# Splitting the last 512 bytes off four large loads of a decode kernel

## The chip, the cores and the metric

The kernel runs on one core of a Trainium2 chip. The core has a matrix engine (PE, with its weight loads shown as PEld), a vector engine (DVE), a scalar engine (ACT), a general engine (POOL) and a sequencer that only issues and waits (SP). Sixteen DMA engines move data between the chip's memory (HBM) and the core's on-chip memory of 128 partitions. A transfer is issued by an instruction on one of the queues and is done when every DMA engine that carries a part of it is done. The metric is the device time of one execution in microseconds; a smaller number is better.

## The reference

One decode step of a transformer block with a modulation vector, for one token, in bfloat16:

```
mod = silu(c) @ w_mod                      # six vectors sa, ca, ga, sb, cb, gb of 512
h = layernorm(x) * (1 + ca) + sa
q = h @ wq                                 # 32 query heads of 128
scores = q . k_cache * 128 ** -0.5         # 8 key heads, each for 4 query heads, 32768 positions
o = softmax(scores) . v_cache
x = x + ga * (o @ wo)
h = layernorm(x) * (1 + cb) + sb
x = x + gb * (relu(h @ w1) @ w2)           # 512 -> 1792 -> 512
```

The caches are the bulk of it: K and V of each of the eight key heads are 32768 x 128 numbers, 8 MB (8192 KB) each, 128 MB in all. The weights add some 15 MB. With a single token there is little arithmetic for each byte.

## The kernel before

**Tiling.** K and V of a head are laid over the 128 partitions so that partition p holds 256 consecutive positions: one row of 32768 numbers, 64 KB, contiguous both in HBM and in its partition. A head's K or V is taken in four steps u = 0 to 3 of 64 positions for each partition. The on-chip memory has a ring of three slots of 64 KB for each partition; a slot holds the K of a head, or the V of a head, or a group of weights (`wmq_sb`, later `tail_sb`).

**The stream.** All large transfers go through SP's queue in one fixed order, the list `stream` (lines 161 to 168): first half of K of head 0, the modulation weights, the weights of q, second half of K of head 0, and then for each head g the K of head g + 1 and the V of head g. The first heads move each K or V whole, in one transfer (`whole`); from K of head 6 on they move in halves, and V of head 7 in a half and two quarters. Then come the output weights in four pieces, w1, and w2 in five. `need(key)` issues the stream up to the piece that is asked for; `load(key)` (line 111) makes the destination and the source of a piece, and `stream_dma` (line 153) issues one transfer. A transfer into a slot that was used before must wait until the readers of its old contents are done.

**One piece in three transfers.** For one piece, the second half of K of head 0 (`UNEVEN`, line 57), `load` issues three transfers in place of one (lines 136 to 141): all 128 rows without their last 512 bytes, then the last 512 bytes of the first 111 rows, then those of the other 17. After V of head 0 it also issues `SPACE` = 14 drain instructions on SP (lines 144 to 146), which do nothing but stand in SP's program.

**The loop.** For each head, DVE transposes K in place in 32 x 32 blocks, eight instructions for each head (line 439), PE multiplies it by a block-diagonal arrangement of q (line 458), the softmax follows (lines 466 to 510), and PE multiplies the weights by V (line 520), for the first heads in a hardware loop on PE. The order on PE and DVE is written out by hand. In the end come the output projection, the second normalisation, w1 (line 761), the relu (line 772), w2 (line 784), two vector operations (lines 789 and 791) and the output transfer (line 792).

**Completion.** Each transfer signals a completion semaphore. There are eight, taken in turn, and in the built program a transfer waits for the one that had its semaphore before it, eight transfers earlier.

Of the kernel before, what the change touches and what calls it, by code (L numbers as in the profile page):

```python
# [17 lines left out]
def kernel(  # L18
# [15 lines left out]
    P = 128  # L34
    _, _, D = A_x.shape
    _, Hkv, Sk, Dh = A_k_cache.shape
# [6 lines left out]
    TK = 64  # L43
# [10 lines left out]

    OUT0, OUT1 = 30, 34

    UNEVEN, EDGE, MOST = ("k", 0, (2, 3)), 2 * TK * Dh - D // 2, 111
    SPACE = 14
    assert Dh == 128 and REP == 4 and D == 512 and FT == W2P[-1][1] and NTILE == 4
    scale = float(Dh) ** -0.5  # L60
    eps = 1e-5
# [8 lines left out]
    def wo_v(i):  # L70
        g0, n = WOP[i]
        return A_wo[g0 * REP * Dh:(g0 + n) * REP * Dh, :].rearrange("(p r) d -> p r d", p=P)
# [32 lines left out]
    def piece(name, at, n):  # L105

        if name not in pieces:
            pieces[name] = ring.tile([P, NTILE * TK * Dh], BF16, tag="slot", name=name)
        return pieces[name][:, at:at + n]

    def load(key):
        kind = key[0]
        if kind == "wm":
            t = piece("wmq_sb", 0, WM).rearrange("p (kt n) -> p kt n", kt=KT)
            src = wm_v
        elif kind == "wq":
            t = piece("wmq_sb", WM, WQ).rearrange("p (kt n) -> p kt n", kt=KT)
            src = wq_v
        elif kind in "kv":
            g, steps = key[1], key[2]  # L120
            src = (kv if kind == "k" else vv)[g, :, TK * steps[0]:TK * (steps[-1] + 1), :]
            name = f"Ksb{g}" if kind == "k" else f"Vsb{g}"
            t = piece(name, TK * Dh * steps[0], TK * Dh * len(steps)).rearrange("p (j d) -> p j d", d=Dh)
        elif kind == "wo":
            g0, n = WOP[key[1]]
            t = piece("tail_sb", g0 * REP * D, n * REP * D).rearrange("p (r d) -> p r d", d=D)
            src = wo_v(key[1])
        elif kind == "w1":
            k0, k1 = W1P[key[1]]
            t = piece("tail_sb", WO + k0 * Dff, (k1 - k0) * Dff).rearrange("p (kt f) -> p kt f", f=Dff)  # L130
            src = w1_v[:, k0:k1]
        else:
            f0, f1 = W2P[key[1]]
            t = piece("tail_sb", WO + KT * Dff + f0 * D, (f1 - f0) * D).rearrange("p (f d) -> p f d", d=D)
            src = w2_v[:, f0:f1]
        if key == UNEVEN:
            row, src_row = (x.rearrange("p j d -> p (j d)") for x in (t, src))
            for rows, cols in (
                (slice(0, P), slice(0, EDGE)), (slice(0, MOST), slice(EDGE, None)), (slice(MOST, P), slice(EDGE, None)),
            ):  # L140
                stream_dma(row[rows, cols], src_row[rows, cols])
        else:
            stream_dma(t, src)
        if key[:2] == ("v", 0):
            for _ in range(SPACE):
                nc.sync.drain()
        if kind in "kv":
            for i, u in enumerate(steps):
                loaded[(kind, g, u)] = t[:, TK * i:TK * (i + 1), :]
        else:  # L150
            loaded[key] = t

    def stream_dma(dst, src):
        i = nc.sync.dma_start(out=dst, in_=src)  # L154
        tc.stamp_issue_order_token(i.ins, "sp_stream")
        if last_loop:

            tc.add_manual_dep(i.ins, last_loop[0], mybir.DependencyInfo(
                mybir.DependencyClass.NoSync, mybir.DependencyReason.DATA))
# [11 lines left out]
    def need(key):  # L171
        while key not in loaded:
            load(stream[pos[0]])
            pos[0] += 1
        return loaded[key]
# [457 lines left out]
    with tc.manual_schedule(engines={mybir.EngineType.PE, mybir.EngineType.DVE}):  # L633
# [143 lines left out]
        for part, (f0, f1) in enumerate(W2P):  # L777
            w2_sb = need(("w2", part))
            for ft in range(f0, f1):
                for i in (0, 2, 1, 3):  # L780
                    row = OUT0 + i
                    to, w = (0, 32) if row < 32 else (32, OUT1 - 32)
                    at = 32 * ft + 31 - (row - to)
# [39 lines left out]
```

## Time and profile before

| what | value |
|---|---|
| time, median of 3 runs | 354.37 us (354.33 to 354.50) |
| span of the profiled execution, first to last instruction | 352.6 us |
| PE busy | 277.9 us, 79% |
| DVE busy | 201.0 us, 57% |
| ACT busy | 25.1 us, 7% |
| bytes read from HBM | 149.42 MB, 424 GB/s over the span |

The profile is of one execution. It gives that execution's span and no separate time; the span lies 1.77 us below the median of the runs. A busy engine here is one that executes an instruction; issuing a transfer and waiting are not counted. DMA shares are of all sixteen engines; in a narrow window a packet is counted with its whole duration in the window in which it starts, so such a share can be over 100%. A "packet" is what one DMA engine moves in one piece: here one row of a transfer, or a message of a few bytes that signals completion. Loads of the program's own code appear as queues of the kind "instruction".

### The profile page before, as it was taken

What the parts mean: (1) busy time and instruction counts of PE and PEld (TensorE: products, weight loads), DVE (VectorE), ACT (ScalarE), POOL (GpSimd) and SP (SyncE); (2) the same over time, 40 slices, a digit from 0 to 9 for tenths busy, and PEclk for the clock granted to TensorE, in tenths of its full rate; (3) what the DMA queues carried; (4) which work ended last, traced back from release to release, by engine and by line L of the source; (5) the groups of instructions that cost most, each with busy time, mean ns of one, the idle gap of its engine ahead of it and who ended that gap; (6) DMA issues with size and microseconds to landing.
All of it is one profiled execution on the core that took longest, in us unless ns stands there. A gap on an engine that the chain in (4) does not pass through costs nothing. (4 is left out here: it accounts for less than half of the span.)

```text
span 352.6 us, 3715 instructions
## 1 busy us (share of the span) xinstructions
PE 277.9 (79%) x1310; PEld 113.5 (32%) x1310; DVE 201.0 (57%) x226; ACT 25.1 (7%) x69; POOL 3.1 (1%) x15
## 2 busy tenths in 40 slices
PE   0065891895998599976998499968999799989994
PEld 0021330331333234322333134323444233434442
DVE  6663564984079614974099506975684257744142
ACT  1200103002000200001000200011000100011000
POOL 2000000000000000000000000000000000000000
PEclk9999897798999879998999879996999989999999
DMA  9999989999999999999999999999999999999995
GB/s 357 398 435 452 472 388 461 454 394 454 461 394 448 439 424 439 424 433 439 416 446 446 409 440 461 411 394 454 431 414 435 457 417 420 444 439 409 425 425 214
DMA packets 5224, 149.59 MB, mean 424 GB/s; under 512 B 604, under 2 KB 988, under 8 KB 1628
## 3 DMA queue, kind: packets, MB, share of 16 engines
q1 hardware_dynamic: 5180, 149.43, 98.5%
q8 instruction: 8, 0.13, 0.1%
q14 instruction: 4, 0.03, 0.0%
q10 hardware_dynamic: 32, 0.00, 0.0%
HBM read 149.42 MB, written 0.00 MB: 424 GB/s over the span
## 5 line engine op out<-in xcount | busy, mean ns | idle before, releaser
L439 DVE STREAM_TRANSPOSE Ksb<-Ksb 128x2048 f32<-128x2048 f32 x60 | 133.1, 2276 | 60.2 <-DMA Ksb<-in_A_k_cache_dram 60.2
L520 PE MATMUL o_ps<-Vsb,P_g 128*16 (+1 forms) x512 | 127.0, 408 | 13.0 <-ACT P_g L495 10.0
L458 PE MATMUL S_ps<-Ksb,qbd 128*128 128x512 bf16 x512 | 120.4, 386 | 10.9 <-DVE Ksb L439 9.3
L458 PEld LDWEIGHTS <-qbd 128*128 128x128 bf16 x512 | 49.6, 98 | 78.1 <-issue 21.8
L520 PEld LDWEIGHTS o_ps<-Vsb,P_g 128*16 x352 | 34.0, 97 | 67.8 <-issue 36.5
L520 PEld LDWEIGHTS <-P_g 128*16 128x16 bf16 x160 | 13.8, 90 | 19.0 <-issue 0.4
L420 ACT COPY qbd<-qrep_sb 32x16 bf16<-32x16 bf16 x32 | 6.4, 201 | 175.2 <-PE S_ps L458 174.1
L500 DVE STREAM_TRANSPOSE P_g<-P_g 128x1024 bf16<-128x1024 bf16 x8 | 10.0, 1245 | 14.1 <-ACT P_g L495 14.1
L471 DVE TENSOR_REDUCE m_p<-S_ps 128x1 f32<-128x1024 f32 x7 | 8.6, 1223 | 13.3 <-PE S_ps L458 13.3
L322 PE MATMUL mod_ps<-wmq_sb,siluT 128*1 128x512 bf16 x24 | 3.6, 624 | 9.9 <-DMA wmq_sb<-in_w_mod_dram 9.9
L331 DVE STREAM_TRANSPOSE Ksb<-Ksb 128x2048 f32<-128x2048 f32 x4 | 8.9, 2280 | 1.6 <-DMA Ksb<-in_A_k_cache_dram 1.6
L476 PE MATMUL mT_ps<-ident_f,m_p 128*1 128x128 f32 x8 | 2.2, 270 | 8.9 <-DVE m_p L471 7.9
L495 ACT ACTIVATE P_g<-S_ps,nbias 128x1024 bf16<-128x1024 f32 x8 | 8.9, 1114 | 0.2
L506 PE MATMUL L_ps<-Lexp,ones_f 128*128 128x4 f32 x16 | 3.1, 263 | 6.3 <-DVE Lexp L503 4.3
L492 ACT ACTIVATE nbias<-Mb_ps 128x1 f32<-128x1 f32 x8 | 1.4, 171 | 88.3 <-PE Mb_ps L490 88.3
L509 DVE RECIPROCAL Linv<-L_ps 128x4 f32<-128x4 f32 x8 | 1.3, 164 | 10.9 <-PE L_ps L506 10.9
L252 PE MATMUL xc_ps<-cx_sel,wmq_sb 16*128 16x2 bf16 x4 | 0.3, 172 | 8.7 <-DVE wmq_sb L246 8.7
L555 PE MATMUL acc_ps<-mask_sb,Y 16*128 16x4 f32 x16 | 3.0, 258 | 4.9 <-DVE Y L551 4.9
L548 DVE TENSOR_TENSOR o_ps<-o_ps,smask 16x512 f32<-16x512 f32 x8 | 5.3, 668 | 2.8 <-PE o_ps L520 2.8
L586 DVE CAST o_sb<-o_ps 128x4 bf16<-128x4 f32 (+2 forms) x4 | 0.7, 165 | 10.3 <-PE o_ps L582 10.3
L506 PEld LDWEIGHTS L_ps<-Lexp,ones_f 128*128 128x128 f32 x16 | 2.6, 203 | 9.6 <-issue 5.6
L551 DVE TENSOR_REDUCE Y<-o_ps 16x128 f32<-16x512 f32 x8 | 5.4, 678 | 0.3
(116 smaller groups left out, 82.8 us busy)
## 6 DMA issues: line engine op xcount, KB each, us to landing
Ksb<-in_A_k_cache_dram SPq DMA_DIRECT2D x5, 4096.0 KB, 23.5
Vsb<-in_A_v_cache_dram SPq DMA_DIRECT2D x5, 4096.0 KB, 38.0
wmq_sb<-in_A_wq_dram SPq DMA_DIRECT2D x1, 4096.0 KB, 28.0
Vsb<-in_A_v_cache_dram SPq DMA_DIRECT2D x2, 2048.0 KB, 38.1
Ksb<-in_A_k_cache_dram SPq DMA_DIRECT2D x1, 4032.0 KB, 37.1
wmq_sb<-in_w_mod_dram SPq DMA_DIRECT2D x1, 3072.0 KB, 18.8
tail_sb<-in_A_wo_dram SPq DMA_DIRECT2D x1, 2048.0 KB, 23.0
tail_sb<-in_B_w_dram SPq DMA_DIRECT2D x1, 1792.0 KB, 30.4
```

The source lines that it names most:

```text
L322: nc.tensor.matmul(dst[j // 4][32 * (j % 4):32 * (j % 4) + 1, :], lhsT=src_T[:, kt:kt + 1], rhs=w[:, kt, j * 512:(j + 1) * 512], start=(kt ...
L331: nc.vector.transpose(out=t, in_=t)
L420: nc.scalar.copy(out=o, in_=i)
L439: t = nc.vector.transpose(out=KTt.bitcast(F32), in_=KTt.bitcast(F32))
L458: nc.tensor.matmul(S_ps_tiles[g], lhsT=qbd[g % 2][:, hp, 4 * (7 - s):4 * (7 - s) + P], rhs=KTv[:, 16 * sl:16 * sl + 16, h, :, par], start= ...
L471: behind_loop(nc.vector.reduce_max(out=m_p[:], in_=S_g.rearrange("p g f -> p (g f)"), axis=AX.X))
L495: nc.scalar.activation(out=P_g[:], in_=S_g.rearrange("p g f -> p (g f)"), func=ACT.Exp, bias=nbias[:], scale=scale, accum_out=l_g[:],)
L500: behind_loop(nc.vector.transpose(out=P_g[:], in_=P_g[:]))
L506: nc.tensor.matmul(L_ps[:], lhsT=ones_f[:], rhs=Lexp[:], start=True, stop=True)
L520: nc.tensor.matmul(o_tiles[g][:], lhsT=PT, rhs=Vx, start=False, stop=False, skip_group_check=True)
L548: nc.vector.tensor_tensor(out=o, in0=o, in1=smask[:].unsqueeze(2).to_broadcast([16, 4, Dh]), op=ALU.mult,)
L551: nc.vector.tensor_reduce(out=Y[:], in_=o.rearrange("p s d -> p d s"), op=ALU.add, axis=AX.X)
```

## The change

Four whole pieces, K of heads 1 and 2 and V of heads 0 and 1, are treated as the one piece of head 0 already was. Each is issued as one transfer of 128 rows without their last 512 bytes and three transfers of those last 512 bytes: the first 112 rows, and the remaining 16 rows in two parts, 10 and 6, 11 and 5, 12 and 4, or 9 and 7. The second half of K of head 0 keeps its 111 and 17 rows. The drains after V of head 0 go from 14 to 4. The number of bytes does not change; SP issues twelve transfers more.

```
-    UNEVEN, EDGE, MOST = ("k", 0, (2, 3)), 2 * TK * Dh - D // 2, 111
-    SPACE = 14
+    EDGE = D // 2
+    ALL = (0, 1, 2, 3)
+    SPLIT = {
+        ("k", 0, (2, 3)): (111, 17), ("k", 1, ALL): (112, 10, 6), ("v", 0, ALL): (112, 11, 5),
+        ("k", 2, ALL): (112, 12, 4), ("v", 1, ALL): (112, 9, 7),
+    }
+    SPACE = 4
...
-        if key == UNEVEN:
+        if key in SPLIT:
             row, src_row = (x.rearrange("p j d -> p (j d)") for x in (t, src))
-            for rows, cols in (
-                (slice(0, P), slice(0, EDGE)), (slice(0, MOST), slice(EDGE, None)), (slice(MOST, P), slice(EDGE, None)),
-            ):
-                stream_dma(row[rows, cols], src_row[rows, cols])
+            at = len(key[2]) * TK * Dh - EDGE
+            stream_dma(row[:, 0:at], src_row[:, 0:at])
+            r0 = 0
+            for n in SPLIT[key]:
+                stream_dma(row[r0:r0 + n, at:], src_row[r0:r0 + n, at:])
+                r0 += n
         else:
             stream_dma(t, src)
```

## The prediction

> **What bounds the kernel now.** I read the page first, then a table by stage, then the end of the chain of waits. From the page:
>
> ```profile
> span 352.6 us, 3715 instructions
> ...
> q1 hardware_dynamic: 5180, 149.43, 98.5%
> ...
> DMA 19%; PE 5%; DVE 3%; SPq 0%; issue 0%
> ```
>
> SP's queue (q1) carries every large transfer and keeps the sixteen DMA engines occupied for 98.5% of the span. The stage table (span, PE, PEld, DVE, ACT, POOL, granted clock, DMA share, GB/s) shows where the rest is:
>
> ```profile
> 0.00:1.80 1.80, 0.00 (x0) 0.00 (x0) 0.73 (x3) 0.13 (x1) 1.25 (x11) 1.00 0.34 92
> 1.80:40.00 38.20, 14.54 (x86) 5.90 (x87) 20.29 (x50) 5.82 (x16) 1.34 (x5) 0.96 1.02 433
> ...
> 80.00:160.00 80.00, 65.26 (x269) 25.75 (x269) 46.70 (x39) 5.00 (x18) 0.00 (x0) 0.94 1.00 431
> ...
> 345.00:349.30 4.30, 3.40 (x69) 2.01 (x71) 0.71 (x2) 0.47 (x2) 0.00 (x0) 1.00 0.83 326
> 349.30:352.60 3.30, 0.54 (x10) 0.24 (x7) 0.56 (x2) 0.00 (x0) 0.00 (x0) 1.00 0.01 3
> ```
>
> From 1.8 us to 345 us the engines do not pause (shares of about 1.00 at 431 to 433 GB/s), while PE and DVE both have idle time. The end of the chain, in order of time (start, duration, what):
>
> ```profile
> 313.39 25.04 DMA tail_sb<-in_A_wo_dram
> ...
> 338.44 11.14 DMA tail_sb<-in_B_w_dram
> ...
> 349.62 0.29 PE end_ps L784 x4
> ...
> 350.26 0.28 DVE o_bf L791
> ```
>
> The last weights land at 349.58 (338.44 + 11.14) and only about one microsecond of arithmetic and the output follow. A transfer has landed when the slowest of the engines that carry it is done. So the kernel takes a start of about 1.4 us, the work of the most loaded DMA engine, and a fixed end of 3.0 us (349.58 to 352.60). What counts is what the change adds to or takes from one engine's work, and whether it lets the queue run dry. How even the end is, is told by two narrow windows, 348.4 to 349.3 and 348.95 to 349.35 (each with its packet line and its queue line):
>
> ```profile
> DMA packets 134, 0.12 MB, mean 132 GB/s; under 512 B 20, under 2 KB 132, under 8 KB 134
> ...
> q1 hardware_dynamic: 134, 0.12, 38.2%
> ...
> DMA packets 10, 0.01 MB, mean 18 GB/s; under 512 B 3, under 2 KB 10, under 8 KB 10
> ...
> q1 hardware_dynamic: 10, 0.01, 5.5%
> ```
>
> In the last 0.9 us the engines are 38.2% occupied, so they wait 0.56 us on average for the slowest (61.8% of 0.9). In the last 0.4 us the share is 5.5%, less than one engine in sixteen (6.25%): one engine alone finishes last, some 0.3 us behind the rest.
>
> **The change part by part.** Four 8 MB transfers lose the last 512 bytes of each row, and those bytes go in three transfers apiece of 112 rows and two remainders that sum to 16.
>
> *The bytes.* Three windows price a row: 33.5 to 38.3 us, where only the 32,256-byte rows of K of head 0 run; 39.1 to 39.3 us, where only its 111 rows of 512 bytes start; and 39.7 to 40.0 us, inside its 17 rows:
>
> ```profile
> q1 hardware_dynamic: 64, 2.06, 99.5%
> ...
> q1 hardware_dynamic: 26, 0.01, 21.9%
> ...
> DMA packets 13, 0.01 MB, mean 20 GB/s; under 512 B 1, under 2 KB 13, under 8 KB 13
> ...
> q1 hardware_dynamic: 13, 0.01, 6.9%
> ```
>
> The large rows take 0.995 x 4.8 x 16 / 64 = 1.194 us each, so 512 bytes inside a long row cost 1194 x 512 / 32256 = 19.0 ns. A 512-byte row by itself takes 0.219 x 0.2 x 16 / 26 = 27.0 ns. The occupied share 0.219 x 16 = 3.5 is more than the three engines on which I place 111 = 3 x 37 rows, so neighbouring packets overlap a little; counted by starts, three engines start 26 in 0.2 us, one per 23.1 ns each. The third window gives the same for a single engine (13 starts in 0.3 us, 23.1 ns), so 17 rows lie on one engine. Its one packet under 512 bytes, the completion message, is what remains of 0.069 x 0.3 x 16 = 331 ns after 12 x 27.0: 8 ns. Each 512-byte row costs 23.1 ns on a queue that is never empty, and 27.0 ns at most.
>
> *The shares.* 111 rows on three engines and 17 on one fit a rule by which a transfer is cut into equal shares for the largest number of engines up to sixteen that divides its rows. Then 112 rows give every engine seven, and 10, 6, 11, 5, 12, 4, 9 and 7 rows put one row on each of so many engines. If every remainder starts at the same engine, four engines carry 36 short rows in all (28 + 8) and four carry 28, where even shares are 32.
>
> [...] The windows agree with the count (three engines, then one); which engines they are, no run here shows. Cut evenly instead, every engine would have 32 short rows, and the sum below would be its middle value.
>
> *The sum for one engine.* All four transfers together take 32 x 19.0 = 0.606 us of tails off every engine's long rows. Added are, for a lightly loaded engine, 28 x 23.1 = 0.647 us and four completion messages of 8 ns: +0.07 us net. An engine with 32 short rows and eight messages: 0.739 + 0.064 - 0.606 = +0.20 us. The most loaded: 36 x 23.1 = 0.832 and twelve messages, 0.096: +0.32 us. At 27.0 ns a row the three are +0.18, +0.32 and +0.46 us. The bounds are +0.07 and +0.46 us. The page does not name the engine that is last, so I take the middle, +0.20 us. No gain is in it: even the most relieved engine loses four rows (0.09 us) and pays more than that in smaller packets.
>
> *The issues and their waits.* SP's timeline (start, duration to the end of the last in the row, count), with DVE's for the landings of K of head 0's second half, head 1 and head 2:
>
> ```profile
> 2.12 20.99 SPq L154 DMA_DIRECT2D Ksb<-in_A_k_cache_dram  x4
> 35.10 0.35 SPq L154 DMA_DIRECT2D Vsb<-in_A_v_cache_dram  x1
> 52.06 0.33 SPq L154 DMA_DIRECT2D Ksb<-in_A_k_cache_dram  x1
> 79.83 0.33 SPq L154 DMA_DIRECT2D Vsb<-in_A_v_cache_dram  x1
> 102.08 0.33 SPq L154 DMA_DIRECT2D Ksb<-in_A_k_cache_dram  x1
> ...
> 39.25 8.89 DVE L439 STREAM_TRANSPOSE Ksb<-Ksb 128x2048 f32<-128x2048 f32 x4 [3.89 <-DMA Ksb<-in_A_k_cache_dram]
> ...
> 60.18 4.51 DVE L439 STREAM_TRANSPOSE Ksb<-Ksb 128x2048 f32<-128x2048 f32 x2 [0.62 <-DMA Ksb<-in_A_k_cache_dram]
> ...
> 98.77 6.70 DVE L439 STREAM_TRANSPOSE Ksb<-Ksb 128x2048 f32<-128x2048 f32 x3 [13.13 <-DMA Ksb<-in_A_k_cache_dram]
> ```
>
> Twelve issues of 0.33 us are 4 us of SP's own time, free because SP waits most of the span. The built program has eight completion semaphores in turn, and each transfer waits for the one eight places before it. With twelve more transfers these waits fall elsewhere: the short pieces of V of head 0 wait until K of head 0 has landed (39.25, and its 54 short rows on one engine 1.2 us later); the transfer of K of head 2 waits for K of head 1 (60.18, was issued at 52.06); V of head 1 waits for V of head 0, which lands halfway between 60.18 and 98.77, at about 79.5 (was issued at 79.83). Behind each stand the next loads of SP, and DVE's transposes and PE's products wait for these. The cover is the transfer in flight: K of head 2 is needed when V of head 0 ends at 79.5, so its issue at 60.2 has 19 us left, V of head 1 about as much, and K of head 3 is issued at 102 after both. Cost nothing; without that cover, see the second rival. From K of head 3 on the order is as before, and twelve being four beyond eight, the semaphores of the end are only renamed. Ten drains fewer are SP's own idle time.
>
> So 352.60 + 0.20 = 352.80 us of span. The median of the runs, 354.37 us, lies 1.77 us above the profiled span; the forecast is 354.57 us.
>
> **The rivals.** *The end comes together.* If the engine that is last is among the relieved and the short rows cost less than here, the wait of 0.56 us shrinks. Taking all of it, with the +0.07 us of the lightest engine: 353.9 us. For it speaks the lone last engine; against it that only 0.09 us moves.
>
> *The queue runs dry (slower).* The first row of SP's timeline has four issues that last 20.99 us: SP was held, although an issue takes 0.33 us, so the queue can refuse transfers. Now three short transfers stand between K of head 1 and V of head 0. If the queue takes a transfer only when an earlier one has landed, V of head 0, issued at 35.10 before, slips; it decides once that is past 60 us, when K of head 1 is done, or once K of head 2 slips past 79.5. Each dry stretch costs at least the time from an issue to full flow: the first stage moved 92 GB/s for 1.8 us, which is 0.38 us at 433, so flow began at 1.42 us, 0.68 us after the first issue at 0.74 us:
>
> ```profile
> 0.74 0.38 SPq L154 DMA_DIRECT2D Ksb<-in_A_k_cache_dram  x1
> ```
>
> Two such stretches and the forecast's +0.20 give 355.9 us. Against it: the waits for K of head 0 end near 40.5 us, 20 us early.
>
> *Every short transfer stops its engines.* If the 0.68 us were paid for each of the twelve, 8.2 us: 362.7 us. Against it stand the narrow windows, where short rows follow each other without a pause.
> [...]
>
> *An instruction fetch moves.* The program's loads of its own code share these engines; from 346.5 to 348.5 us one cost 3.3% of 16 x 2 us, 1.06 us on one engine:
>
> ```profile
> q8 instruction: 1, 0.02, 3.3%
> ```
>
> The built program has five more PE and four more DVE instructions (extra waits), so fetches shift. One that leaves the last engine gives back the 0.3 us by which it is alone: 354.3 us. One that comes to an engine that ends with the rest adds 1.06 - 0.3 us: 355.3 us.
>
> **How the numbers follow.** Forecast 0.70; ends together 0.06; queue dry 0.12; stopped engines 0.01; fetch 0.07, two thirds of it the cheap side; 0.04 stay for a gain that none of these prices. 0.2% is 0.71 us, about what a measurement of this kernel can tell from no change. The forecast with its bounds (354.44 to 354.83), the ends that come together (0.5 us of gain) and the fetch that leaves lie within it; slower are the dry queue, the stopped engines and the fetch that comes. Faster 0.04, same 0.81, slower 0.15. The range 354.0 to 355.4 takes in the bounds and both fetches and leaves out the dry queue and the last of the evening.
>
> **What would show it.** Right: DMA shares of about 1.00 in all stages from 1.8 to 345 us; 512 packets of 512 bytes and 128 completion messages more on q1 (for each large transfer 16 for its 112 rows and 16 for its remainders), so about 5820 in all; K of head 2 issued at about 60 us, V of head 1 at about 80 us; the last weights landing 0.1 to 0.5 us later; the rest of the end unchanged. Wrong: a stage with a share below 0.97, a landing of K of head 2 after 99.5 us, short rows further apart than 27 ns, or an end in which the engines finish together.

## The result and the profile after

| what | before | after |
|---|---|---|
| time, median of 3 runs | 354.37 us | 355.64 us (355.64 to 355.97) |
| ratio, 95% interval | | 1.0039 (1.0025 to 1.0053) |
| span of the profiled execution | 352.60 us | 353.86 us |
| last weights land (end of the last transfer in the chain) | 349.58 us | 350.18 us |
| from the issue of the output transfer to the end of the span | 2.03 us | 2.69 us |

The change costs 1.27 us; the time lies 0.24 us above the upper end of the predicted range. Two parts of about the same size add up to it: the stream of loads ends 0.60 us later, and the end behind it is 0.66 us longer. Some executions of every kernel, of before too, fall into a slower state (362 to 371 us for before); the medians and ratios in this document leave them out.

The page after, its span, the stream's queue and the shares of the chain:

```profile
span 353.9 us, 3729 instructions
...
q1 hardware_dynamic: 5820, 149.43, 98.2%
...
DMA 19%; PE 5%; DVE 3%; SPq 0%; issue 0%
```

The 640 packets more are the 512 rows and 128 messages that were forecast. Three stages of the table of after:

```profile
80.00:160.00 80.00, 65.31 (x268) 25.50 (x267) 46.28 (x37) 5.16 (x18) 0.00 (x0) 0.94 1.01 435
...
345.00:350.60 5.60, 3.95 (x75) 2.25 (x75) 0.77 (x3) 0.47 (x2) 0.00 (x0) 1.00 0.69 274
350.60:353.90 3.30, 0.00 (x0) 0.00 (x0) 0.51 (x2) 0.00 (x0) 0.00 (x0) 1.00 0.01 3
```

The DMA engines are as full as before (a share of 1.01); the queue did not run dry. SP's timeline of after (start, duration to the end of the last of the row, count):

```profile
2.12 34.33 SPq L161 DMA_DIRECT2D Ksb<-in_A_k_cache_dram  x7
36.58 4.25 SPq L161 DMA_DIRECT2D Vsb<-in_A_v_cache_dram  x4
60.44 1.60 SPq L161 DMA_DIRECT2D Ksb<-in_A_k_cache_dram  x4
80.04 1.55 SPq L161 DMA_DIRECT2D Vsb<-in_A_v_cache_dram  x4
102.41 0.35 SPq L161 DMA_DIRECT2D Ksb<-in_A_k_cache_dram  x1
```

K of head 2 is issued at 60.44 us and V of head 1 at 80.04 us, the forecast's 60 and 80. The end of the chain of after:

```profile
339.04 11.14 DMA tail_sb<-in_B_w_dram
...
350.87 0.28 DVE o_bf L798
```

The last weights land at 350.18 us, 0.60 us later, where the prediction had 0.1 to 0.5 us. The arithmetic behind them is as long as it was. The rest is in the waits of SP, of which after has a row that before does not have (waited for, us in total, times, longest):

```profile
SPq L825 <- DMA out_dram<-o_bf: 0.8, 1, 0.8
```

Line 825 is the program's end. SP passes six waits there, each for two semaphores, in a fixed order. The moments at which it passes them stand in the trace's list of SP's instructions; the star is the wait that holds the output transfer's semaphore:

```
                  output issued   six waits passed                                   span ends
before            350.57          350.91 350.98 351.05  351.50 351.59 351.75*         352.60
after             351.18          351.51 352.35* 352.81 352.89 352.95 353.02          353.86
after, 6 loads    351.06          351.40 351.47 351.93  352.01 352.07 352.24*         353.09
before, 6 loads   350.42          350.76 351.60* 351.67 352.12 352.21 352.27          353.12
after, 14 drains  351.08          351.42 352.26* 352.32 352.38 352.45 352.50          353.34
```

("6 loads" and "14 drains" are experiments below.) Before, the output's semaphore is the sixth. While the output is under way SP passes the other five and sits out a pause of 0.45 us between the third and the fourth; the output lands and 0.85 us later all is over. After, twelve transfers more have turned the eight semaphores on by four: the output's is now the second. Four waits and the pause come when it has landed, 0.67 us (352.35 to 353.02) that were hidden before.

### The profile page after: what moved, and what is told of

Its sections match the earlier page's. It is cut to its first block, busy times and chain, and to the rows that moved or that the text cites. A ratio compares the mean times of both kernels' runs of the same rounds, so it can differ in the third digit from the quotient of the medians.

```text
span 353.9 us, 3729 instructions
## 1 busy us (share of the span) xinstructions
PE 277.8 (78%) x1310; PEld 113.0 (32%) x1310; DVE 201.0 (57%) x226; ACT 25.1 (7%) x69; POOL 3.1 (1%) x15
```

## The experiments

The ratios are against runs of the kernel before on the same chip, with 95% intervals.

### The end: the place of the output's semaphore, and the drains

Four small transfers more, early and on another queue, turn the semaphores on by four:

```
-        nc.scalar.dma_start(out=cx_row[8 * i:8 * i + 8], in_=row.rearrange("(a n) -> a n", a=8))
+        for r0, r1 in ((0, 4), (4, 6), (6, 8)):
+            nc.scalar.dma_start(
+                out=cx_row[8 * i + r0:8 * i + r1], in_=row.rearrange("(a n) -> a n", a=8)[r0:r1],
+            )
```

In the changed kernel that brings the output's semaphore back to the last place:

> The changed kernel, with the two small loads of the modulation vector on the scalar engine's queue cut in three each: four transfers more, early on, in another queue; the large stream is the same. The completion semaphores are taken in turn, so the output transfer gets another one of the eight, the one that the program's end waits for last instead of second. Theory A (0.6 us of the loss lie in the DMA stream and 0.66 us in the end, because of the place of the output's semaphore in the order of the final waits): the span from the issue of the output transfer to the end goes from 2.72 back to about 2.03 us, and the time from 355.64 to about 354.97 us; the last weights still land about 0.6 us later than before the change. Rival B (the end is longer for the later landing or the longer program, not for the semaphore): 2.72 us stay, 355.64 us.

Measured: 354.91 us, ratio 1.0022 (1.0007 to 1.0036); the output is issued at 351.06 and the span ends at 353.09, 2.02 us. In the kernel before it takes the semaphore to the second place:

> The kernel before, with the same six small loads in place of two. The large stream is that of before; the output's semaphore moves from the place that is waited for last to the one waited for second. Theory A: the last weights land as before (349.6 us), the span from the issue of the output transfer to the end goes from 2.03 to about 2.7 us, and the time from 354.37 to about 355.03 us. Rival B (the semaphore does not matter): 354.37 us, within 0.1.

Measured: 354.98 us, ratio 1.0018 (1.0009 to 1.0028). Its stream ends as early as before's (349.44 us), but the end costs what it costs after, and the same wait appears:

```profile
SPq L821 <- DMA out_dram<-o_bf: 0.8, 1, 0.8
```

```profile
350.42 0.29 SPq L795 DMA_DIRECT2D out_dram<-o_bf  x1
```

From 350.42 to 353.12 are 2.70 us, where before has 2.03. One edit that touches no weight gains 0.7 us in one kernel and loses 0.6 us in the other. The times alone are close to their noise; what decides is the end of the traces: 2.02 and 2.03 us in both kernels where the output's semaphore is the last, 2.69 and 2.70 us where it is the second. Theory A holds for the end, rival B falls.

The fourteen drains back in the changed kernel:

```
-    SPACE = 4
+    SPACE = 14
```

> The changed kernel with its 14 drains on SP in place of 4; transfers, their order and their semaphores are those of the changed kernel. The end has six waits and a stall of SP of 0.42 us between two of them. Theory A1 (the stall sits at a fixed place of SP's program, such as a load of its next part): with ten more instructions ahead it falls before the landing of the output, where it is hidden, and the time goes from 355.64 to about 355.2 us. Theory A2 (the stall belongs to the waits on these semaphores): 355.64 us, with the stall at the same wait.

Measured: 355.14 us, ratio 1.0034 (1.0018 to 1.005). The list above has no pause among its six waits any more, and the end takes 2.26 us. The pause stands earlier now, between two groups of loads. SP's timeline, first of after, then with fourteen drains:

```profile
313.61 1.75 SPq L161 DMA_DIRECT2D tail_sb<-in_A_wo_dram  x4
315.41 23.96 SPq L161 DMA_DIRECT2D tail_sb<-in_B_w_dram  x6
```

```profile
313.52 1.75 SPq L161 DMA_DIRECT2D tail_sb<-in_A_wo_dram  x4
315.70 23.58 SPq L161 DMA_DIRECT2D tail_sb<-in_B_w_dram  x6
```

From the end of the first row to the start of the second are 0.05 us in after and 0.43 us here. Counted in the list of SP's instructions, the pause follows the 79th in all five kernels of the table above and in the even variant below: it belongs to a place in SP's program, and ten drains more move that place out of the end. After has a load of 8 KB of program code behind 349 us, which starts at 353.44 us:

```profile
q14 instruction: 1, 0.01, 0.3%
```

With fourteen drains there is none behind 349 us; it starts at 319.64 us. In both the load comes behind the pause, which ends at 352.81 and at 315.70 us. That SP's own program is loaded in the pause was the author's estimate; no run shows it, and what SP does there stays open.

### The stream: what a shorter row saves, and what short rows cost

The first theory for the stream was that a row of 65,024 bytes is hardly cheaper than one of 65,536. Even shares first:

```
-        ("k", 0, (2, 3)): (111, 17), ("k", 1, ALL): (112, 10, 6), ("v", 0, ALL): (112, 11, 5),
-        ("k", 2, ALL): (112, 12, 4), ("v", 1, ALL): (112, 9, 7),
+        ("k", 0, (2, 3)): (111, 17), ("k", 1, ALL): (112, 16), ("v", 0, ALL): (112, 16),
+        ("k", 2, ALL): (112, 16), ("v", 1, ALL): (112, 16),
```

> The changed kernel with the last 512 bytes of the four pieces in two transfers of 112 and 16 rows in place of three: every DMA engine has 32 short rows and 8 messages instead of 28 to 36 and 4 to 12, and eight transfers more than before the change leave the output's semaphore where it was, last. Theory A (a long row shortened by 512 bytes saves only about 12 ns, a short row with its message costs 24 to 30 ns): the end is 2.03 us again, the stream 0.40 to 0.45 us longer than before the change, time 354.8 us. By the prediction's price of 19.0 ns for 512 bytes of a long row: +0.20 us, 354.57 us. If the four extra transfers and the unevenness cost nothing and all comes from the end: 354.4 us.

Measured: 354.81 us, ratio 1.0011 (1.0002 to 1.002), on the 0.4 us of Theory A. Against the first experiment, which has up to 36 short rows and 12 messages on an engine and the same short end, its median is 0.10 us lower; four rows and four messages are 4 x 23.1 + 4 x 8 = 124 ns. That would fit if the engine that ends last is one of the most loaded, but it is not shown: the intervals overlap, and in the profiled executions the even variant's last weights land later (350.17 us) than those of the first experiment (350.08 us).

The shortening by itself, in the kernel before (line 141). The last 512 bytes of ten pieces are not loaded here but set to zero, so this kernel leaves out a part of K and V:

```
+        elif kind in "kv" and len(key[2]) == NTILE:
+            row, src_row = (x.rearrange("p j d -> p (j d)") for x in (t, src))
+            stream_dma(row[:, 0:NTILE * TK * Dh - D // 2], src_row[:, 0:NTILE * TK * Dh - D // 2])
+            nc.gpsimd.memset(row[:, NTILE * TK * Dh - D // 2:], 0.0)
         else:
             stream_dma(t, src)
```

> The kernel before, with all ten 8 MB transfers (K of heads 1 to 5, V of heads 0 to 4) cut by the last 512 bytes of each row, and those bytes not loaded at all but set to zero on the general engine, which leaves out a part of K and V. No transfer is added, the completion semaphores are those of before. Each DMA engine has 80 long rows that are 512 bytes shorter. What does the shortening alone save? By the prediction's price of 19.0 ns a row 1.52 us: 352.88 us. Theory A (a row of 65,024 bytes takes only 12.4 ns less than one of 65,536): 0.99 us, 353.41 us. If the zeroing delays the stream, the transfers will show it by being issued later.

Measured: 353.02 us, ratio 0.9958 (0.9944 to 0.9971): 1.49 us of 354.5, or 18.6 ns a row. The end of its chain:

```profile
337.10 11.13 DMA tail_sb<-in_B_w_dram
```

The last weights land at 348.23 us, 1.35 us earlier than before. The theory of the cheap shortening fell here, and the prediction's 19.0 ns stood. In the packets of the trace a row of 65,536 bytes has a median of 2.418 us and one of 65,024 bytes 2.399 us. The even variant's 0.4 us had to come from elsewhere: its rows of 65,024 bytes have the same median, but some are slower, and their mean between 30 and 122 us is 2.419 us.

Twice as many pieces in the even variant, to see whether the price is steady:

```
-        ("k", 2, ALL): (112, 16), ("v", 1, ALL): (112, 16),
+        ("k", 2, ALL): (112, 16), ("v", 1, ALL): (112, 16), ("k", 3, ALL): (112, 16), ("v", 2, ALL): (112, 16),
+        ("k", 4, ALL): (112, 16), ("v", 3, ALL): (112, 16),
```

> Tails of 112 and 16 rows for eight pieces (K of heads 1 to 4, V of heads 0 to 3) in place of four: sixteen transfers more than before the change, so the output's semaphore is again the last one waited for. Twice the rows, twice the messages. Theory A (a steady price for each piece, 0.10 us as the even variant showed): +0.82 us on 354.4, 355.2 us. By the prediction's prices (0.20 us for four): +0.40 us, 354.8 us. Rival (the 0.4 us are paid once, by something that the first split shifts, such as a code load): 354.8 us too, but then with the same time between later landings as in the even variant.

Measured: 355.30 us, ratio 1.0031 (1.0016 to 1.0045), 0.8 us for eight pieces against 0.4 us for four, so it is paid for each piece. And longer pieces cut off in the even variant:

```
+    CUT = {("v", 0, ALL): 2 * EDGE, ("k", 2, ALL): 4 * EDGE, ("v", 1, ALL): 8 * EDGE}
...
-            at = len(key[2]) * TK * Dh - EDGE
+            at = len(key[2]) * TK * Dh - CUT.get(key, EDGE)
```

> The even variant with other cuts: K of head 1 by 512 bytes, V of head 0 by 1024, K of head 2 by 2048, V of head 1 by 4096. Theory A1 (a cut row has a fixed extra cost of about 6.5 ns, whatever its cut): rows of 64,512, 63,488 and 61,440 bytes take 2.384, 2.346 and 2.270 us, and the time stays that of the even variant, 354.8 us. Theory A2 (bytes at the end of a long row are cheap, 12.4 ns for each 512): the rows take 2.390, 2.365 and 2.316 us, the pieces cut off cost more than they save, and the time is about 355.3 us.

Measured: 357.95 us, ratio 1.0103 (1.0088 to 1.0118), far beyond both. Medians of the rows are again in proportion (61,440 bytes: 2.267 us), but some take up to 3.4 us, and rows of 4096 bytes up to 0.38 us in place of 0.16. Its stage table (span, PE, PEld, DVE, ACT, POOL, clock, DMA share, GB/s):

```profile
100.00:120.00 20.00, 17.67 (x78) 7.13 (x76) 18.01 (x10) 0.80 (x4) 0.00 (x0) 1.00 1.06 415
```

The engines are fuller and move less than in the stage of after above (1.06 at 415 GB/s against 1.01 at 435).

### Where the short rows hold up the long ones

First the reading side, with the long cuts and with the even variant:

```
-                stream_dma(row[r0:r0 + n, at:], src_row[r0:r0 + n, at:])
+                cut = len(key[2]) * TK * Dh - at
+                tail = src_row[:, at:] if key[1] == 0 and kind == "k" else src.rearrange(
+                    "p j d -> (p j d)")[0:P * cut].rearrange("(p e) -> p e", e=cut)
+                stream_dma(row[r0:r0 + n, at:], tail[r0:r0 + n])
```

> The variant with cuts of 512, 1024, 2048 and 4096 bytes (357.95 us), but its short rows are read from consecutive addresses at the beginning of the same K or V in place of the ends of rows that lie 65,536 bytes apart; they are written to the same places on the chip, with the same number and sizes, so the tails of four pieces hold other numbers. Theory H (short rows that lie a whole row apart in HBM hold up the long rows of the other engines that run at the same time): the slow long rows disappear, and what is left is the price of the packets, 354.4 + 0.2 = 354.6 us. Rival (short rows of such sizes slow their neighbours wherever they are read from, for instance where they are written): 357.9 us as before.

> The even variant (four pieces, 112 and 16 rows of 512 bytes; 354.81 us) with the short rows read from consecutive addresses in the same way, so that the tails of four pieces hold other numbers. Theory H: the last long row of each engine in a piece, which is 40 to 80 ns slow in the changed kernel, takes its usual 2.40 us, and the time is what the prediction's prices give, 354.4 + 0.20 = 354.6 us. Rival (it is the small packets, not their addresses): 354.8 us, and long rows of up to 2.48 us stay at each of the four pieces.

Measured: 357.89 us (1.0102, 1.0087 to 1.0117) and 354.89 us (1.0017, 1.0009 to 1.0026). Theory H fell: where the short rows are read does not matter. Then the four pieces cut into whole rows, 112 and 16, with no short rows at all:

```
-            stream_dma(row[:, 0:at], src_row[:, 0:at])
+            if key[1] == 0 and kind == "k":
+                stream_dma(row[:, 0:at], src_row[:, 0:at])
+            else:
+                at = 0
```

> The four pieces cut by rows and not by columns: two transfers of 112 and 16 whole rows of 65,536 bytes, no short rows, four transfers more than before; with the six small loads on the scalar engine's queue, so that the output's semaphore is the last one waited for. Theory H (short rows slow the long rows): no slow long rows, four completion messages more on each engine, 0.03 us: 354.4 to 354.5 us. Rival (any change of transfer inside a piece costs each engine some 60 ns): +0.25 us, 354.7 us.

Measured: 437.08 us, ratio 1.2369 (1.2319 to 1.2419). Neither theory had this. A stretch in which one of the four pieces is loaded:

```profile
100.00:110.00 10.00, 0.78 (x4) 0.22 (x2) 3.56 (x6) 2.18 (x7) 0.00 (x0) 0.69 1.25 190
```

The engines are full and move 190 GB/s. Rows of 65,536 bytes take mostly 3 to 5 us in the transfers of 112 rows; where those of 16 rows run, the median is 8.8 us and the longest row 9.6 us. What is left is which rows are written at one time, and four kernels test it. The tails go in one transfer of 128 rows (with the cuts of 512 bytes, then with the long ones), or whole rows go in two halves of 64:

```
-        ("k", 0, (2, 3)): (111, 17), ("k", 1, ALL): (112, 10, 6), ("v", 0, ALL): (112, 11, 5),
-        ("k", 2, ALL): (112, 12, 4), ("v", 1, ALL): (112, 9, 7),
+        ("k", 0, (2, 3)): (111, 17), ("k", 1, ALL): (128,), ("v", 0, ALL): (128,),
+        ("k", 2, ALL): (128,), ("v", 1, ALL): (128,),
...
-                stream_dma(row[r0:r0 + n, at:], src_row[r0:r0 + n, at:])
+                some = slice(r0, r0 + n) if at else slice(r0 // n, P, 2)
+                stream_dma(row[some, at:], src_row[some, at:])
```

The last three lines make the even and the odd rows of the whole-row variant, which has (64, 64) in place of (128,). Its other form has the rows 0 to 63 in one transfer and 64 to 127 in the next.

> Four pieces cut by 512 bytes, each with its tails in one transfer of 128 rows in place of 112 and two remainders; the six small loads keep the output's semaphore last. Theory P (partitions): in a transfer of 128 rows every DMA engine writes the same eight partitions as in the long transfers, so no long row is slowed; what is left is 32 x 23.1 + 4 x 8 - 32 x 19.0 = 0.16 us, 354.3 to 354.4 + 0.16 = about 354.5 us. Rival (short rows slow long rows wherever they go): 354.75 us, with about 16 slow long rows at each piece.

> The cuts of 512, 1024, 2048 and 4096 bytes that took 357.95 us, with the tails in one transfer of 128 rows each. Theory P: about 354.5 us, and no row of 61,440 bytes above its usual 2.27 us by more than 0.1. Rival: 357.9 us.

> The four pieces in two transfers of 64 whole rows: the even rows, then the odd rows. [...] Theory P: 354.4 us, as before the change, where 112 and 16 whole rows took 438.6 us. Rival (whole rows in transfers of fewer than 128 rows are slow as such): 400 us or more.

> [...] Theory P: at least twice the time for these four pieces, 4 x 19.3 = 77 us more, about 430 us. Rival (the slow rows came from the transfer of 16 rows alone): 354.4 us.

Measured: 354.71 us (1.0014, 1.0005 to 1.0023), 354.54 us (1.0012, 1.0003 to 1.002), 354.34 us (1.0000, 0.9992 to 1.0009) and 440.43 us (1.2437, 1.2421 to 1.2453). The long cuts lose 3.4 us when their tails go in one transfer of 128 rows, and the stage reads like an undisturbed one:

```profile
100.00:120.00 20.00, 17.53 (x78) 7.12 (x76) 17.98 (x12) 0.80 (x4) 0.00 (x0) 1.00 1.00 429
```

Two halves of whole rows cost nothing when they are the even and the odd rows, and half the bandwidth when they are rows 0 to 63 and 64 to 127. First the even and odd rows, then the halves:

```profile
40.00:60.00 20.00, 14.01 (x62) 5.89 (x60) 11.60 (x10) 3.46 (x8) 0.00 (x0) 0.93 0.98 424
60.00:80.00 20.00, 16.84 (x65) 7.02 (x66) 17.89 (x11) 0.00 (x0) 0.00 (x0) 0.79 1.03 446
```

```profile
40.00:60.00 20.00, 15.15 (x62) 6.15 (x60) 11.00 (x9) 3.46 (x8) 0.00 (x0) 0.84 0.98 202
60.00:80.00 20.00, 0.56 (x2) 0.50 (x2) 1.47 (x3) 0.00 (x0) 0.00 (x0) 0.50 1.02 210
```

Both have full engines; with the halves they move 202 to 210 GB/s. SP's timeline shows the same for V of head 1 and K of head 3, first with even and odd rows, then with the halves:

```profile
80.62 1.11 SPq L165 DMA_DIRECT2D Vsb<-in_A_v_cache_dram  x2
102.83 0.36 SPq L165 DMA_DIRECT2D Ksb<-in_A_k_cache_dram  x1
```

```profile
101.77 1.10 SPq L164 DMA_DIRECT2D Vsb<-in_A_v_cache_dram  x2
141.81 0.36 SPq L164 DMA_DIRECT2D Ksb<-in_A_k_cache_dram  x1
```

The step from the one to the other is 40 us with the halves and 22 us without. The data, the rows, their lengths and the number of transfers are the same; only which rows go together differs. For the short rows that leaves the writing side, since reading them from elsewhere changed nothing (357.89 against 357.95 us, 354.89 against 354.81 us). For whole rows the order of reading changes together with the order of writing, and no run separates the two.

Where 16 whole rows run, a row takes 3.6 to 4.0 times as long as before (8.8 and 9.6 against 2.418 us), and the halves move 202 to 210 GB/s where the even and odd rows move 424 to 446. Theory P named the partitions that an engine writes. That was the author's assumption: no run here shows how the rows of such a transfer are shared out or where an engine writes, and the 77 us that the expectation for the halves adds up rest on it. What the runs show is that 128 short rows in one transfer, and whole rows as even and odd ones, slow next to nothing (0.03 to 0.05 us on each engine, in the list below), and that the halves cost 86 us.

How much this comes to in each kernel shows in the long rows of the trace between 50 and 122 us, where the four pieces end. The excess over the median of their length, of rows more than 15 ns slow, summed and divided by sixteen engines:

```
                              rows over 15 ns slow   excess for each engine
before                        1                      0.03 us
after                         67                     0.30 us
after, 6 small loads          62                     0.23 us
even (112, 16)                63                     0.23 us
even, read contiguously       72                     0.23 us
tails left out                37                     0.14 us
tails of 128 rows             1                      0.03 us
even and odd whole rows       5                      0.04 us
cuts up to 4096 bytes         89                     2.37 us
the same, tails of 128 rows   11                     0.05 us
```

With the cuts of 512 bytes in 112 rows and a rest, about as many slow rows as there are engines stand at the end of each of the four pieces; with tails of 128 rows there are none. They are not the only slow rows. The kernel without the tails has 37, most of them away from the ends of pieces, and between 38 and 43 us, at K of head 0, some executions have 0.2 to 0.3 us more on each engine, among them one of two with the same stream (the changed kernel with 14 drains, but not with 4). Where these come from stays open.

In time, the gain of 128 rows is clear for the long cuts alone, 3.4 us. For the cuts of 512 bytes the median is 0.39 us above before, and the even variant's was 0.42 us above its own, although the slow rows are gone and the expectation was 0.16 us. The runs spread from 354.43 to 355.18 us, half of them above 354.8 us, and the profiled execution took 354.60 us. Why half of the runs were slower stays open.

### An attempt to move a load of code away from the last engine

Two groups of three matmuls that only keep PE busy were left out (`keep_clock(3)`, lines 749 and 766 of the kernel before), to have PE's last load of code come later:

```
-        keep_clock(3)
         layernorm_T(x1T[:], stat2, h2T[:], modT_sb[:, 3 * KT:4 * KT], ncb[:], "ln2", meanwhile)
...
-        keep_clock(3)
         hidT = room("tail_sb", TAIL, [P, 512])[:, 0:NQ].rearrange("p (f e) -> p f e", e=32)
```

> The kernel before without two groups of three matmuls that PE only runs to stay busy (ahead of the second normalisation and ahead of the relu). Twelve instructions fewer in PE's program, so PE reaches its next load of program code later. If the 16 KB load near 348 us thereby comes after the engine that it slows has carried its last weights, the last weights land about 0.3 us earlier (349.3) and the time is 354.1 us. Rival: the load still comes ahead of the last weights, or PE then waits for its code: 354.4 us or up to 355. If PE's clock falls without these matmuls, the arithmetic after the last weights gets longer instead.

Measured: 355.12 us, ratio 1.0015 (1.0006 to 1.0025). Its last stages:

```profile
345.00:349.30 4.30, 3.31 (x48) 2.06 (x50) 0.71 (x2) 0.47 (x2) 0.00 (x0) 0.52 0.80 313
349.30:352.60 3.30, 1.52 (x30) 1.25 (x24) 0.56 (x2) 0.00 (x0) 0.00 (x0) 0.50 0.00 0
```

The granted clock of PE is 0.52 where before had 1.00, and the chain of waits ends on the matmuls on w2 in place of the landing:

```profile
347.65 3.19 PE end_ps L782 x54
...
350.87 0.29 DVE o_rows L787
```

The last of the expectation's three cases came true. The first did not: the 16 KB load is still there ahead of the last weights, at 347.7 us where before has it at 347.9 us. Its row between 346 and 352 us:

```profile
q8 instruction: 1, 0.02, 1.4%
```

No kernel of the study that does the whole work beats the one before.

## Why the prediction was wrong

**What bounds the kernel: right.** The stream of loads sets the end. Its shares of about 1.00 stayed, no stage ran dry, and a later last landing went into the time in full.

**The bytes: right.** 512 bytes of a long row are 18.6 ns (19.0 forecast), and short rows keep a median of 27.0 ns in all kernels with cuts of 512 bytes.

**The shares: right in count, but the middle was chosen.** The prediction gave the most loaded engine +0.32 us and took +0.20 us because the page does not name the last engine. The count shows in the messages. In the trace of before the 111 rows end with three and the 17 with one, and SP's 35 transfers of 128 rows have 16 each and the output's of 4 rows has four (568 in all); in after each of the four pieces cut has 48 messages at its end, 16 for the long rows and 32 for its 112 rows and remainders. The prediction's own rows held a hint. In before one of the three engines carries the 17 rows too: the first of them starts at 39.745 us, right behind the message at 39.739, and that engine is back at its long rows at 40.15 us, the other two at 39.61 and 39.63. In after the packets of the engine with these 54 short rows, followed by their times, are 7, 1 and 1 short rows at each of the four pieces: it carries 36 and is one of the most loaded. If that engine is the last, 0.12 us were too little; no run shows which engine it is.

**The sum for one engine: a term was missing.** It priced the short rows on their own engine only. Where the tails go in 112 rows and remainders, long rows that are still under way on other engines are slower: 0.27 us on each engine (0.30 less the 0.03 that before has). That the slow rows go when the tails go in one transfer of 128 rows is shown by the trace (0.03 us, as before); what the cuts of 512 bytes gain by it in time is not. The sign of it stood in the trace of before: when the 111 and 17 rows of K of head 0 run there, thirteen long rows, as many as there are engines without short ones, are 51 to 66 ns slow. 0.32 + 0.27 = 0.59 us, and the landing moved by 0.60 us. That closeness is luck: with the same stream it moved by 0.50 us with the six small loads and 0.52 us with the fourteen drains, and two executions with the stream of before land 0.14 us apart (349.58 and 349.44).

**The issues and their waits: right up to the end.** K of head 2 and V of head 1 were issued when forecast, and the cover held. The step that failed is near its close: "twelve being four beyond eight, the semaphores of the end are only renamed". They are renamed, but the program's end waits for them in a fixed order, and the output's name decided how much of that order lay behind its landing: 0.66 us. The fixed end of 3.0 us was an end for one place of the output's semaphore. Without it the time would have lain within the predicted range: the changed kernel with the output's semaphore back in the last place took 354.91 us. That the drains cost nothing was wrong with it: in the place that the output's semaphore now has, fourteen hide the pause (355.14 against 355.64 us).

**The sum that the runs give**: 0.32 + 0.27 + 0.66 = 1.25 us on the span of 352.60, against 353.86 measured. The last term is shown by the experiments; the first two are the best account of the rest, and each is uncertain by some 0.1 us.

**The rivals.** The dry queue would have given 355.9 us, near the result, but for a reason that did not occur. The engines that pause 0.68 us for each short transfer did not occur either, and the ends did not come together. The load of code near 348 us only moved along with the stream, from 347.9 to 348.4 us. No rival and no end of the range had the order of the final waits in it.

## What to carry to other kernels

Count the transfers of the whole program when one is added: the completion semaphores are taken in turn, and where the end waits for them in a fixed order, the output's should be the last (2.03 us from its issue to the end here, 2.69 us where it was the second). Which rows go together in a transfer that follows a long one closely is worth a run: with the long cuts, tails of 128 rows took 354.54 us, tails of 112 and 16 rows 357.95 us. Read GB/s beside the DMA share: a share of 1.00 stood beside 429 GB/s, one of 1.02 beside 210 GB/s, so the share does not tell full engines from held-up ones. For the price of a packet, look at the mean and the longest in the neighbouring transfers too, not at its own rows alone.

## What was not expected of the hardware

Whole rows of 64 KB in two transfers cost nothing or 86 us (354.34 and 440.43 us), by which rows go together. With cuts of up to 4096 bytes whose tails go in 112 and 16 rows, slow long rows came to 2.37 us on each engine, while the kernel with its tails in 128 rows had next to none (0.05 us). And where six matmuls were left out of PE's idle time, its granted clock was half for the last 7.6 us (0.52 and 0.50 against 1.00).
